# First loads of a fused attention and feed-forward kernel dealt out anew over two DMA queues

## The chip, the cores and the metric

The kernel runs on one core of a Trainium2 chip. The metric is the device time of one execution in microseconds; lower is better. Three runs of the kernel before the change gave 213.14, 213.52 and 213.74 us, so the median is 213.52 us.

## What is computed

A sequence of 2048 rows with 512 columns in bf16 is normalized row by row. The normalized rows go two ways. One is a sliding attention with 32 heads of 16 columns, where each row looks at itself and at 7 earlier rows at steps of 2. The other is a gated feed-forward layer with 1792 inner columns. The result is the input plus the attention's output times the silu of the feed-forward's output.

```python
xn = _layernorm(x, axis=-1)                      # x: 1 x 2048 x 512
s = _A_ref(xn, A_wqkv, A_wo)                     # q, k, v = xn @ wqkv; 8 keys per row; ... @ wo
g = _silu(_B_ref(xn, B_w_gate, B_w_up, B_w_down))  # (gelu(xn @ w_gate) * (xn @ w_up)) @ w_down
return x + s * g
```

## The kernel before

The 2048 rows are worked on in four blocks (j = 0 to 3) of 512 rows; a block has four tiles of 128 rows. For each block the kernel normalizes and transposes the rows (xnT), makes q, k and v, multiplies q with the shifted keys on VectorE (logits), takes the softmax, multiplies with the shifted values on VectorE, passes the result o through DRAM to turn it around (line 989 on), and multiplies it with wo (s_ps, line 1021). Beside that TensorE makes g and u (line 900) and y (line 960) of the feed-forward part. All matmuls of blocks 1 to 3 have 512 columns; those of q, k and v of block 0 are made tile by tile with 128 columns (`qkv_tiles`, line 584), so that they can begin when the first 128 rows are there.

**How the order of the work comes about.** Nothing is put in order by the hardware. Each step is an `Op` with an engine, an estimated duration, the names of the steps that it needs (a "~" in front means: needs only the start of that one) and a priority. `schedule` (line 126) plays the program through with fixed estimates of durations and of DMA times, always takes the step that can begin first, and among those within 0.05 us the one with the lowest priority. The order found this way is the order of the instructions on each engine. The numbers in `PARAMS` (base priorities N, S, V, Q, F, Y, O for the blocks and one `nudge` for each step) move the priorities, so other numbers give another order of the same steps.

**The first loads.** `loads` (line 1106) makes a list of DMAs, each of which may only be issued after the one before it in the list. SyncE (SP) issues all of them but three, which ScalarE's (ACT's) sequencer issues. In order: tile 0's rows in two column halves (ld_x0_0a on SP, ld_x0_0b on ACT), tile 1's rows in two column halves (both on SP), wq in two halves of 256 KB (ld_wqa and ld_wq, both on ACT), wk in two halves (ld_wka and ld_wk, both on SP), tiles 2 and 3 in one DMA of 256 KB (ld_x2_0, SP), wv in two halves (SP), and then, all on SP, the rows of block 1, the gate and up weights, and the rest. Below, "wka" and "wkb" are the first and the second half of wk, and the same for wq.

**The start of block 0.** Tiles 0 and 1 are normalized in column halves by `early_tile`: statistics (line 429), their sum (432), the root on ScalarE (435), reciprocal (440), the two normalized halves (444), two transposes each on TensorE (452), and copies out of PSUM (459 and 461). Then TensorE multiplies tile 0 with the first half of wq ("q0a", 8 matmuls), with the second ("q0b"), with wka ("k0a") and with wkb ("k0b"); tile 1's q ("q1a", "q1b") is cut in the same way, and all other tiles take 16 matmuls in one step. `preset` (line 264) is a square root of one column that ScalarE runs early, so that the table of that function is loaded before the first root needs it; it may not come ahead of the start of ld_wqa. `warm` (line 254) runs matmuls on zeros until the first rows are there.

**The end of blocks 0 to 2.** For a whole block at once, VectorE multiplies s16 (the evacuated s_ps) with the silu (line 1046), a DMA issued by GpSimd adds x (line 1049), and two DMAs of 256 KB, issued by SP, write the result to DRAM (line 1055). There is one buffer s16; block 1 can write into it (line 1036) when block 0's stores have read it.

Of the kernel before, what the change touches and what calls it, by code (L numbers as in the profile page):

```python
# [16 lines left out]
P = 128  # L17
# [4 lines left out]
TQ = 512  # L22
# [7 lines left out]
B, S, D, DF = 1, 2048, 512, 1792  # L30
NC = D // P
NF = DF // P
NJ = S // TQ
TPB = TQ // P
# [26 lines left out]
    sums=(3,), psum=(0,), warm=4, slack=3.5, N=[267.5, 33.2, 480.8, 875.4], S=[194.3, -690.4, 43.8, -317.7],  # L61
    V=[-45.5, -104.1, 270.7, -195.0], Q=[-3.6, -356.0, 73.8, 32.5], F=[86.8, 80.1, 275.5, 543.3],
    Y=[-111.3, 10.6, -115.3, -110.9], O=[33.1, -472.0, -324.1, 458.9], vnorm=(), vcopy=(2,), vsum=(0,),
    crowd=1.35,
    nudge=[
# [162 lines left out]
class Kernel:  # L228
# [33 lines left out]
    def preset(self):  # L262

        self.op("preset", "ACT", 0.2, ["warm0", "~ld_wqa"], lambda: self.nc.scalar.activation(
            out=self.spare[:], in_=self.eps[:], func=AF.Sqrt), prio=-1e6, table="sqrt")
# [16 lines left out]
    def layernorm(self, j):  # L282
        base = self.when("N", j)
        for tt in range(TPB):
            t = j * TPB + tt
# [89 lines left out]
            else:  # L375
                self.op(f"stats{t}", "DVE", 0.61,
                        [f"ld_x{j if j else 2}_{j}"] + {2: ["copy1"], 3: ["~aggr2"]}.get(t, ["~rstd3"]), stats, prio=prio,
# [631 lines left out]
    def out(self, j):  # L1009
# [32 lines left out]
        if j < NJ - 1:  # L1042
# [9 lines left out]

            def store(i, j=j):
                a = j * TQ + i * 2 * P
                self.nc.sync.dma_start(
                    out=self.out2d[a : a + 2 * P, :].rearrange("(t p) d -> p t d", p=P),
                    in_=self.t[f"s16{j}"][:, 2 * i : 2 * i + 2, :],
                )
# [5 lines left out]
            for i in range(2):  # L1064
                self.op(f"store{j}_{i}", "SP", 0.35, [f"add{j}"], lambda i=i, f=store: f(i), use=[f"s16{j}"],
                        nbytes=P * TPB * D, kind="out")
# [39 lines left out]
    def loads(self, src):  # L1106
        A_x, A_wqkv, A_wo, w_gate, w_up, w_down = src

        def x_tile(t, a=0, b=D, eng="sync"):
            getattr(self.nc, eng).dma_start(  # L1110
                out=self.x_sb[:, t, a:b], in_=A_x[0][t * P : (t + 1) * P, a:b]
            )
# [6 lines left out]
        def w_qkv(i, a=0, b=NC, eng="sync"):  # L1119
            getattr(self.nc, eng).dma_start(  # L1120
                out=self.w_sb[i][:, a:b, :],
                in_=A_wqkv.rearrange("(k p) n -> p k n", p=P)[:, a:b, i * D : (i + 1) * D],
            )
# [11 lines left out]
        def w_o():  # L1135
# [3 lines left out]
        kb = 1024  # L1139
        early = [(f"ld_x{t}_0{'ab'[i]}",  # L1140
                  lambda t=t, i=i: x_tile(t, i * D // 2, (i + 1) * D // 2, "sync" if t or not i else "scalar"),
                  64 * kb if t else kb) for t in range(2) for i in range(2)]
        h = NC // 2
        wq = [("ld_wqa", lambda: w_qkv(0, 0, h, "scalar"), 256 * kb), ("ld_wq", lambda: w_qkv(0, h, NC, "scalar"), 256 * kb)]
        wk = [("ld_wka", lambda: w_qkv(1, 0, h), 256 * kb), ("ld_wk", lambda: w_qkv(1, h, NC), 256 * kb)]
        wv = [("ld_wva", lambda: w_qkv(2, 0, h), 256 * kb), ("ld_wv", lambda: w_qkv(2, h, NC), 256 * kb)]
        x23 = [("ld_x2_0", lambda: x_block(2, 4), 256 * kb)]
        xb = [(f"ld_x{j}_{j}", lambda j=j: x_block(j * TPB, (j + 1) * TPB), 512 * kb) for j in range(NJ)]
        seq = early + wq + wk + x23 + wv + [xb[1]]
# [124 lines left out]
```

## Time and profile before

| What | Value |
|---|---|
| Median of three runs | 213.52 us (213.14 to 213.74) |
| The profiled execution's own time | 213.6 us |
| Its span, first to last instruction | 211.8 us |
| TensorE (PE) busy | 206.1 us |
| VectorE (DVE) busy | 187.6 us |
| ScalarE (ACT) busy | 150.3 us |
| GpSimd (POOL) busy | 65.5 us |
| Granted TensorE clock, mean | 0.999 |

The span is the time between the first and the last instruction of the profiled execution; 1.8 us of its time lie around it. PE's weight loads (PEld) run beside the matmuls. A row of the timeline gives start, duration, engine, line of the kernel, operation, what is written and read, and how many instructions are merged in it; a "q" behind the engine's name marks a DMA that the engine's sequencer issues, and such a row's duration is that of issuing, not of the transfer. A row of the DMA view gives the size of one transfer and the time from issue to landing.

### The profile page before, as it was taken

The page shows a single profiled execution, that of the slowest core. Times are in us where ns is not written, and L with a number is a line of the kernel's source. Part 1 is how long each engine was busy: PE and PEld are TensorE (multiplying, and loading weights), DVE is VectorE, ACT ScalarE, POOL GpSimd, SP SyncE. Part 2 cuts the span into 40 slices and gives each one's busy share as a digit, 9 for nine tenths or more (in the row PEclk, how much of TensorE's full clock was granted, in tenths as well). Part 3 has the DMA queues.
Part 4 walks back from the last instruction along what each step waited for, and adds up shares of the span by engine and source line. Part 5 has one row for each costly group of instructions (what it writes and reads, how often), then busy time and mean ns, then how long its engine had stood idle before and what let it go on. Part 6 is the DMA issues. An engine that isn't in the chain of part 4 may idle for free.

```text
span 211.8 us, 3074 instructions
## 1 busy us (share of the span) xinstructions
PE 206.1 (97%) x1105; PEld 102.0 (48%) x1123; DVE 187.6 (89%) x218; ACT 150.3 (71%) x257; POOL 65.5 (31%) x107
## 2 busy tenths in 40 slices
PE   7999999999999999999999999999999999999994
PEld 2896443445444444444444444444444444444442
DVE  4788998869999998999999999999999999997024
ACT  3587957999999899766905489966614489859051
POOL 5034200002115787440459520479730011001000
PEclk9999999999999999999999999999999999999999
DMA  5999999203802888962898865358797069708903
GB/s 182 348 382 373 298 280 240 50 3 74 173 25 73 186 135 144 178 192 38 144 114 135 166 173 115 99 99 162 143 192 163 0 104 231 163 0 149 249 4 99
DMA packets 33119, 32.17 MB, mean 152 GB/s; under 512 B 17088, under 2 KB 29648, under 8 KB 33104
## 3 DMA queue, kind: packets, MB, share of 16 engines
q0 software_dynamic: 5136, 14.41, 35.8%
q1 hardware_dynamic: 27136, 16.95, 31.0%
q10 hardware_dynamic: 832, 0.62, 1.0%
q8 instruction: 9, 0.15, 0.3%
q14 instruction: 6, 0.05, 0.1%
HBM read 14.12 MB, written 6.31 MB: 96 GB/s over the span
## 4 chain that ended last, share of the span: by engine, by line
PE 94%; DMA 2%; SPq 1%; issue 1%; DVE 0%; ACT 0%
PE g_ps L900 23%; PE y_ps L960 23%; PE u_ps L900 23%; PE qkv_ps L500 15%; PE s_ps L1021 6%; PE qkv_ps L584 5%; DMA wk_sb<-in_A_wqkv_dram 2%; SPq L1110 1%; PE L_ps L716 0%; PE tr_ps L345 0%; SPq L1120 0%; DVE s L1076 0%; ACT sil L976 0%; DVE s L1082 0%
## 5 line engine op out<-in xcount | busy, mean ns | idle before, releaser
L900 PE MATMUL g_ps<-xnT,wg_sb 128*128 128x512 bf16 x221 | 54.2, 379 | 0.2
L900 PE MATMUL u_ps<-xnT,wu_sb 128*128 128x512 bf16 x217 | 52.7, 379 | 0.3
L960 PE MATMUL y_ps<-wd_sb,hT 128*128 128x512 bf16 (+2 forms) x233 | 51.4, 366 | 0.2
L916 ACT ACTIVATE gl<-g_ps 128x512 bf16<-128x512 f32 x56 | 32.6, 598 | 18.6 <-PE g_ps L900 10.8
L772 POOL DMA_DIRECT2D Ls<-prod x48 | 36.3, 844 | 29.0 <-DMA Ls<-prod 9.8
L677 DVE TENSOR_TENSOR prod<-q_sb,k_sb 128x2048 bf16<-128x2048 bf16 x32 | 38.0, 1216 | 0.7 <-ACT q_sb L515 0.7
L924 ACT ACTIVATE hT<-u_ps 128x512 bf16<-128x512 f32 x56 | 32.4, 601 | 7.2 <-PE u_ps L900 6.6
L843 DVE TENSOR_TENSOR pv<-attn,v_arr 128x4096 bf16<-128x4096 bf16 x16 | 36.1, 2283 | 0.0
L960 PEld LDWEIGHTS <-hT 128*128 128x128 bf16 x238 | 22.8, 98 | 25.9
L900 PEld LDWEIGHTS <-wu_sb 128*128 128x128 bf16 x224 | 21.8, 98 | 26.6 <-issue 0.4
L900 PEld LDWEIGHTS <-wg_sb 128*128 128x128 bf16 x224 | 21.9, 98 | 26.2
L938 DVE TENSOR_TENSOR hT<-hT,gl 128x1024 bf16<-128x1024 bf16 x28 | 18.8, 683 | 1.3 <-ACT gl L916 1.1
L691 DVE TENSOR_TENSOR prod<-prod 128x2048 bf16<-128x2048 bf16 x16 | 19.2, 1214 | 0.0
L1021 PE MATMUL s_ps<-wo_sb,oT_sb 128*128 128x512 bf16 (+2 forms) x68 | 15.1, 366 | 0.1
L976 ACT ACTIVATE sil<-y_ps 128x512 bf16<-128x512 f32 (+2 forms) x17 | 9.1, 576 | 8.6 <-PE y_ps L960 8.5
L850 DVE TENSOR_TENSOR pv<-pv 128x2048 bf16<-128x2048 bf16 x12 | 14.3, 1215 | 0.0
L649 POOL DMA_DIRECT2D v_arr<-vT_dram x16 | 10.9, 700 | 10.4 <-DMA vT_dram<-vst 10.0
L866 POOL DMA_DIRECT2D pv<-pv x4 | 3.6, 894 | 30.6 <-DVE pv L843 30.1
L515 ACT ACTIVATE q_sb<-qkv_ps 128x512 bf16<-128x512 f32 x12 | 7.1, 624 | 8.2 <-PE qkv_ps L500 8.2
L1036 ACT ACTIVATE s<-s_ps 128x512 bf16<-128x512 f32 x15 | 8.9, 602 | 5.4 <-PE s_ps L1021 5.4
L500 PE MATMUL qkv_ps<-xnT,wv_sb 128*128 128x512 bf16 x48 | 12.3, 379 | 0.0
L542 POOL DMA_DIRECT2D vT_dram<-vst x12 | 7.2, 605 | 15.7 <-ACT vst L522 15.7
(91 smaller groups left out, 231.9 us busy)
## 6 DMA issues: line engine op xcount, KB each, us to landing
Ls<-prod POOLq DMA_DIRECT2D x48, 128.0 KB, 3.7
v_arr<-vT_dram POOLq DMA_DIRECT2D x16, 142.0 KB, 4.2
vT_dram<-vst POOLq DMA_DIRECT2D x16, 128.0 KB, 3.6
pv<-pv POOLq DMA_DIRECT2D x4, 512.0 KB, 5.4
oT_dram<-o_sb SPq DMA_DIRECT2D x16, 128.0 KB, 3.4
oT_sb<-oT_dram SPq DMA_DIRECT2D x4, 512.0 KB, 4.8
wg_sb<-in_B_w_gate_dram SPq DMA_DIRECT2D x2, 896.0 KB, 10.6
wu_sb<-in_B_w_up_dram SPq DMA_DIRECT2D x2, 896.0 KB, 12.5
```

The lines of the kernel that those rows point to most:

```text
L500: self.nc.tensor.matmul(ps[:], lhsT=self.w_qkv(which, dk, c), rhs=self.t[f"xT{j}"][:, dk, :], start=(dk == 0), stop=(dk == NC - 1),)
L677: self.nc.vector.tensor_tensor(out=self.t[pair][:, c % 2].rearrange("p n w t -> p w n t"), in0=q.unsqueeze(1).to_broadcast([P, W, 2, P]), ...
L691: self.nc.vector.tensor_tensor(out=pr[:, 0], in0=pr[:, 0], in1=pr[:, 1], op=ALU.add)
L772: self.nc.gpsimd.dma_start(out=self.t[f"Ls{j}"][H * tq : H * (tq + 1)], in_=self.t[f"pr{j}_{tq // 2}_0"][s::NC, 0, tq % 2], **(dict(accum_ ...
L843: self.nc.vector.tensor_tensor(out=pv[:], in0=self.t[f"at{j}"][:, 2 * i : 2 * i + 2, :].unsqueeze(2).to_broadcast([P, 2, DH, P]), in1=win, ...
L850: self.nc.vector.tensor_tensor(out=pv[:, 0], in0=pv[:, 0], in1=pv[:, 1], op=ALU.add)
L900: nc.tensor.matmul(ps[:], lhsT=w[:, dk, fc * P : (fc + 1) * P], rhs=self.t[f"xT{j}"][:, dk, :], start=(dk == 0), stop=(dk == NC - 1),)
L916: self.nc.scalar.activation(out=self.t[f"gl{j}_{pair}"][:, fc % 2, :], in_=self.t[f"ps_g{j}_{fc}"][:], func=AF.Gelu_apprx_tanh,)
L924: self.nc.scalar.activation(out=self.t[f"h{j}"][:, fc, :], in_=self.t[f"ps_u{j}_{fc}"][:], func=AF.Copy)
L938: self.nc.vector.tensor_tensor(out=h, in0=h, in1=self.t[f"gl{j}_{pair}"][:], op=ALU.mult)
L960: nc.tensor.matmul(self.t["ps_" + key][:, 0 : n1 - n0], lhsT=self.t[f"h{j}"][:, fc, tt * P : (tt + 1) * P], rhs=self.wd_sb[:, fc, n0:n1], ...
L1021: self.nc.tensor.matmul(ps[:, 0 : n1 - n0], lhsT=self.t[f"oT{j}"][:, c, tt * P : (tt + 1) * P], rhs=self.wo_sb[:, c, n0:n1], start=(c == 0 ...
```

## The change

Four things are changed.

1. The list of first loads: tile 1's halves go one to each queue, and so do the two halves of wq and of wk. The second half of wq moves from ACT to SP, and the first half of wk from SP to ACT. Tiles 2 and 3 are loaded by two DMAs of 128 KB in place of one of 256 KB, and tile 2's and tile 3's statistics each wait for their own.
2. `preset` may not come ahead of the start of ld_x1_0b (tile 1's second half, now on ACT) in place of ld_wqa.
3. Block 0's result is stored by one DMA of 512 KB in place of two of 256 KB; blocks 1 and 2 keep two.
4. All the numbers in `PARAMS` that set priorities are new: the base priorities, `slack` (3.42 for 3.5) and the whole list of nudges, so that the order of the steps can differ anywhere.

The estimates in `schedule` and the steps themselves are otherwise the same.

```diff
-    sums=(3,), psum=(0,), warm=4, slack=3.5, N=[267.5, 33.2, 480.8, 875.4], S=[194.3, -690.4, 43.8, -317.7],
-    V=[-45.5, -104.1, 270.7, -195.0], Q=[-3.6, -356.0, 73.8, 32.5], F=[86.8, 80.1, 275.5, 543.3],
-    Y=[-111.3, 10.6, -115.3, -110.9], O=[33.1, -472.0, -324.1, 458.9], vnorm=(), vcopy=(2,), vsum=(0,),
+    sums=(3,), psum=(0,), warm=4, slack=3.42, N=[236.5, 17.4, 498.7, 880.9], S=[216.5, -699.2, 31.7, -311.4],
+    V=[-49.3, -109.4, 272.5, -204.7], Q=[2.1, -363.3, 74.7, 33.2], F=[84.5, 80.7, 277.2, 546.4],
+    Y=[-118.9, 11.7, -116.0, -110.2], O=[36.5, -485.8, -342.3, 458.0], vnorm=(), vcopy=(2,), vsum=(0,),
...
-        self.op("preset", "ACT", 0.2, ["warm0", "~ld_wqa"], lambda: self.nc.scalar.activation(
+        self.op("preset", "ACT", 0.2, ["warm0", "~ld_x1_0b"], lambda: self.nc.scalar.activation(
...
-                        [f"ld_x{j if j else 2}_{j}"] + {2: ["copy1"], 3: ["~aggr2"]}.get(t, ["~rstd3"]), stats, prio=prio,
+                        [f"ld_x{j if j else t}_{j}"] + {2: ["copy1"], 3: ["~aggr2"]}.get(t, ["~rstd3"]), stats, prio=prio,
...
+            parts = 2 if j else 1
+            n = TPB // parts
+
             def store(i, j=j):
-                a = j * TQ + i * 2 * P
+                a = j * TQ + i * n * P
                 self.nc.sync.dma_start(
-                    out=self.out2d[a : a + 2 * P, :].rearrange("(t p) d -> p t d", p=P),
-                    in_=self.t[f"s16{j}"][:, 2 * i : 2 * i + 2, :],
+                    out=self.out2d[a : a + n * P, :].rearrange("(t p) d -> p t d", p=P),
+                    in_=self.t[f"s16{j}"][:, n * i : n * (i + 1), :],
                 )
...
+        def half_x(t, i, eng, size=64):
+            return (f"ld_x{t}_0{'ab'[i]}", lambda: x_tile(t, i * D // 2, (i + 1) * D // 2, eng), size * kb)
+
+        def half_w(w, i, eng):
+            return (f"ld_w{'qkv'[w]}" + "a" * (1 - i), lambda: w_qkv(w, i * h, (i + 1) * h, eng), 256 * kb)
+
+        early = [half_x(0, 0, "sync", 1), half_x(0, 1, "scalar", 1), half_x(1, 0, "sync"), half_w(0, 0, "scalar"),
+                 half_x(1, 1, "scalar"), half_w(0, 1, "sync"), half_w(1, 0, "scalar"), half_w(1, 1, "sync")]
+        early += [(f"ld_x{t}_0", lambda t=t: x_tile(t), 128 * kb) for t in (2, 3)]
+        early += [half_w(2, 0, "sync"), half_w(2, 1, "sync")]
```

More of the change, by code (lines that the diff above doesn't have):

```diff
@@ L1063, in out @@
                     nbytes=P * TPB * D * 2, kind="acc")
-            for i in range(2):
+            for i in range(parts):
                 self.op(f"store{j}_{i}", "SP", 0.35, [f"add{j}"], lambda i=i, f=store: f(i), use=[f"s16{j}"],
-                        nbytes=P * TPB * D, kind="out")
+                        nbytes=P * n * D * 2, kind="out")
             return
@@ L1139, in loads @@
         kb = 1024
-        early = [(f"ld_x{t}_0{'ab'[i]}",
-                  lambda t=t, i=i: x_tile(t, i * D // 2, (i + 1) * D // 2, "sync" if t or not i else "scalar"),
-                  64 * kb if t else kb) for t in range(2) for i in range(2)]
         h = NC // 2
[L1144 to L1147, printed above, removed]
+        def half_x(t, i, eng, size=64):
[6 more added lines that the diff above has]
+        early += [half_w(2, 0, "sync"), half_w(2, 1, "sync")]
         xb = [(f"ld_x{j}_{j}", lambda j=j: x_block(j * TPB, (j + 1) * TPB), 512 * kb) for j in range(NJ)]
-        seq = early + wq + wk + x23 + wv + [xb[1]]
+        seq = early + [xb[1]]
         seq += [("ld_wga", lambda: w_ff(w_gate, lambda: self.wg_sb, 0, half), 896 * kb)]
```

88 rows, old and new, of the table nudge are left out of this document.

## The prediction, made before the changed kernel ran

> **What bounds the kernel now.** I read the head of the page first, then the busy time by stages, then the chain of waits in order of time, and last the timeline of the stages that the change touches.
>
> ```profile
> span 211.8 us, 3074 instructions
> ...
> PE 206.1 (97%) x1105; PEld 102.0 (48%) x1123; DVE 187.6 (89%) x218; ACT 150.3 (71%) x257; POOL 65.5 (31%) x107
> ...
> PE 94%; DMA 2%; SPq 1%; issue 1%; DVE 0%; ACT 0%
> ```
>
> PE is busy for 97% of the span and holds 94% of the chain that ended last. The stages say where the rest is; the columns are stretch, its length, busy time (and instructions) of PE, PEld, DVE, ACT and POOL, granted clock, busy share of the DMA engines, GB/s.
>
> ```profile
> 3.00:5.00 2.00, 2.00 (x8) 0.65 (x6) 1.91 (x7) 0.52 (x3) 1.00 (x10) 1.00 0.99 308
> 5.00:6.50 1.50, 1.28 (x13) 0.99 (x13) 1.27 (x6) 0.67 (x2) 0.00 (x0) 1.00 1.00 309
> 6.50:8.00 1.50, 1.40 (x24) 1.23 (x22) 0.53 (x3) 0.60 (x1) 0.00 (x0) 1.00 1.04 352
> ...
> 18.00:100.00 82.00, 81.58 (x379) 37.91 (x385) 77.59 (x87) 70.86 (x125) 25.88 (x38) 1.00 0.69 149
> 100.00:195.00 95.00, 94.53 (x434) 43.66 (x441) 94.00 (x86) 64.47 (x104) 34.44 (x46) 1.00 0.68 129
> 195.00:205.00 10.00, 9.95 (x49) 4.62 (x48) 0.05 (x1) 2.76 (x5) 0.00 (x0) 1.00 0.58 152
> ```
>
> From 18 to 205 us PE idles 0.42 + 0.47 + 0.05 = 0.94 us in all. No order of the steps can win more than that there, so a gain has to come from the start or the end. The chain shows both:
>
> ```profile
> 2.68 5.27 DMA wk_sb<-in_A_wqkv_dram
> ...
> 8.00 3.31 PE qkv_ps L584 x56
> ...
> 208.46 0.29 ACT sil L976
> ...
> 209.09 0.23 DVE s L1082
> ```
>
> The last thing that PE waits for is wkb: issued at 2.68, landed at 2.68 + 5.27 = 7.95 us; from 8.00 us on it is PE's own work to the end. The end (silu, gate, add, store from 208.46 us) isn't touched by the change.
>
> ```profile
> 5.78 1.45 PE L584 MATMUL qkv_ps<-xnT,wq_sb 128*128 128x128 bf16 x16 [0.22 <-ACT xnT L459]
> 7.07 0.61 PE L584 MATMUL qkv_ps<-xnT,wk_sb 128*128 128x128 bf16 x8
> 7.51 0.39 PE L452 MATMUL tr_ps<-ident,xn 128*128 128x128 bf16 x4
> ...
> 8.47 0.61 PE L584 MATMUL qkv_ps<-xnT,wq_sb 128*128 128x128 bf16 x8
> ...
> 10.26 1.06 PE L584 MATMUL qkv_ps<-xnT,wv_sb 128*128 128x128 bf16 x16
> ```
>
> Starts tell the pace better than the modelled ends. Eight matmuls of 128 columns take 7.51 - 7.07 = 0.44 us and four transposes half of that, 0.22; so the transposes are through at 7.73, and PE stands still until 8.00: **0.27 us**. That is all that an earlier wk can win, against 213.6 us of this execution. The 16 matmuls of q0 take 7.07 - 5.78 = 1.29 us where 16 at the later pace take 0.89, so 0.4 us go there to a slower PE, though the granted clock reads 1.00. The Trainium skill ("TensorE: Matmul & The Clock Gate", Part 1) has matmuls at half pace until a free-running activity window of about 3.4 us has passed; by that rule these 0.4 us could shrink or grow by a few tenths with the window's phase, without any cause in the change.
>
> **The change part by part: the loads.** Here are issues and landings of before; a DMA row's last number is the time to landing.
>
> ```profile
> 0.82 1.34 SPq L1110 DMA_DIRECT2D x_sb<-in_A_x_dram  x3
> 1.81 0.43 ACTq L1120 DMA_DIRECT2D wq_sb<-in_A_wqkv_dram  x1
> 2.20 0.94 SPq L1120 DMA_DIRECT2D wk_sb<-in_A_wqkv_dram  x2
> 3.19 0.47 SPq L1115 DMA_DIRECT2D x_sb<-in_A_x_dram  x1
> ```
>
> ```profile
> x_sb<-in_A_x_dram SPq DMA_DIRECT2D x1, 64.0 KB, 3.2
> wq_sb<-in_A_wqkv_dram ACTq DMA_DIRECT2D x1, 256.0 KB, 3.8
> wk_sb<-in_A_wqkv_dram SPq DMA_DIRECT2D x1, 256.0 KB, 4.1
> x_sb<-in_A_x_dram SPq DMA_DIRECT2D x1, 256.0 KB, 5.3
> ```
>
> The three SP issues of x take 1.34 us, so x1's second half goes out at about 1.73 and lands 3.2 later, near 4.9. wqb lands at 1.81 + 3.8 = 5.6, wka at 2.20 + 4.1 = 6.3, tiles 2 and 3 at 3.19 + 5.3 = 8.5 us. These landings follow the order of issue across both queues, not two streams side by side. From 3 to 8 us the 16 DMA engines are busy all the time (shares 0.99, 1.00, 1.04). So bytes ahead of a load decide: x0, x1, wq and wk are 128 + 128 + 512 + 512 = 1280 KB, and all of these lie ahead of the end of wk before and after. **wkb gains nothing: 7.95 us as before.** The Trainium skill ("DMA: Bandwidth & Descriptors", section "Issuing engines are not separate DMA queues") says the same: DMAs issued from several engines run on the same 16 engines, and only issue time is saved; by that the change's dealing out wins 0 us, and if it were wrong the sum would be rival 1 below. The busy shares agree.
>
> **wka loses.** Before, its 256 KB went ahead of wkb's. Now wka is ACT's fourth DMA, one issue behind its third (1.81 + 0.43, so about 2.25), and wkb is SP's fourth (2.20, the place that wka had): both go out together, share the engines, and land at nearly one time. Bounds for wka: 6.3, as before, and 7.95, as wkb. Both compete over the whole stretch, so I take a value near the later end, **7.6**. PE then idles from 7.07 until 7.6. If it stays with the order k0a, transposes of tile 1, k0b, q1a: k0a 7.65 to 8.10, transposes to 8.32, k0b to 8.77, and q1a begins at 8.77 in place of 8.47: +0.30. If the new priorities put the transposes first, they lie in the gap, and 16 matmuls from 7.65 end at 8.54: +0.07. Bounds: with wka at 7.95 and the old order 8.00 + 0.44 + 0.22 + 0.44 = 9.10, so +0.63; with wka at 6.3 and wkb early enough, -0.27. I take **+0.2**, between the two orders.
>
> **x1's second half** moves behind wqa and beside wqb: 768 KB lie ahead of its end, where wqb was before (5.6). So it lands between 4.9 and 5.6 us.
>
> ```profile
> 5.02 0.42 DVE L429 BATCH_NORM_STATS2 stats<-x_sb 128x6 f32<-128x256 bf16 x1
> ...
> 6.25 0.60 DVE L444 TENSOR_SCALAR xn<-x_sb,mv,rstd 128x256 bf16<-128x256 bf16 x2
> ...
> 7.83 0.49 DVE L461 COPY xnT<-tr_ps 128x256 bf16<-128x256 bf16 x2 [0.97 <-PE tr_ps L452]
> 8.48 0.69 DVE L291 BATCH_NORM_STATS2 stats<-x_sb 128x6 f32<-128x512 bf16 x1 [0.16 <-DMA x_sb<-in_A_x_dram]
> ```
>
> At worst tile 1's statistics begin at 5.6 in place of 5.02, the normalized halves end at 6.85 + 0.6 = 7.45 in place of 6.85. Before, the transposes began at 7.51 only because PE was at k0a, so 7.45 is still early enough: **0**. Behind the waiting statistics on DVE stands tile 0's second copy, for q0b, which PE reaches in the second half of its 1.29 us; should it come up to 0.3 us late there, PE's wait for wka behind it takes that up. **Tiles 2 and 3 apart**: one SP issue more (0.47 us), but SP has six issues ahead of wv before and after, so wv isn't later. Tile 2's 128 KB land some 0.35 us earlier (half of 256 KB at 352 GB/s), so DVE's 0.16 us of waiting at 8.48 goes; PE takes tile 2 only behind the row of 10.26, with work that is there: **0**.
>
> **preset** and ACT's fourth issue:
>
> ```profile
> 1.74 1.28 ACT L264 ACT_TABLE_LOAD   x1 [1.74 <-PEq L1258]
> ...
> 3.04 0.20 ACT L264 ACTIVATE spare<-eps 128x1 f32<-128x1 f32 x1
> 3.98 0.29 ACT L435 ACTIVATE rstd<-mv,eps 128x1 f32<-128x1 f32 x1 [0.74 <-DVE mv L432]
> ```
>
> The table load moves behind one more issue of 0.43 us: 2.2 to 3.5, the root of one column to 3.7. The first root waits for DVE until 3.98, so 0.74 us of cover shrink to 0.3: **0**. If preset slipped by a further issue, 0.15 us of it would delay all that follows.
>
> **Block 0's store in one.**
>
> ```profile
> 124.34 0.90 SPq L1055 DMA_DIRECT2D out_dram<-s  x2
> 150.71 4.35 SPq L993 DMA_DIRECT2D oT_dram<-o_sb  x4
> ```
>
> ```profile
> L1036 ACT ACTIVATE s<-s_ps x4: 597/597/597, 168.1 to 171.1; 128x512 bf16<-128x512 f32 x4
> ```
>
> One issue of 0.45 us goes. SP has nothing to do until 150.71, and s16 is written again only at 168.1: **0**, with tens of us of cover.
>
> **The new priorities** change the order everywhere; no row of before shows the new one. Above: at most the 0.94 us of idle time can go. Below: what a badly timed step costs is rival 2. I take 0, nearest to the rows, since the same estimates of durations that made the order of before left 0.94 us idle in 187.
>
> **Sum**: 213.6 + 0.2 = 213.8 us for an execution like the profiled one, which lies 0.08 above the median of 213.52; so **213.7 us**. A difference under 0.3%, 0.64 us, is about what a measurement here can't tell from none.
>
> **The rivals.** *1. Two queues do bring wk earlier.* Should both halves be there at 7.07 to 7.7 us, the 0.27 us go: 213.3. For it: DMA moves 308 GB/s from 3 to 5 us and 352 later, so the early stretch has some slack. Against it: the full shares, and landings in order of issue.
>
> *2. The new order makes VectorE late (slower).* DVE is 99% busy from 100 to 195 us, so a delay before that isn't made up.
>
> ```profile
> 189.15 1.22 DVE L855 TENSOR_TENSOR o_sb<-pv 128x2048 bf16<-128x2048 bf16 x1
> ...
> 195.69 0.37 SPq L1002 DMA_DIRECT2D oT_sb<-oT_dram  x1
> ...
> 203.26 2.75 PE L1021 MATMUL s_ps<-wo_sb,oT_sb 128*128 128x512 bf16 x12
> ```
>
> ```profile
> DMA to landing us min/median/max: 4.7/4.7/4.7
> ```
>
> The last attention block is done on DVE at 190.4; it is turned through DRAM and back at 195.69 + 4.7 = 200.4, and PE takes it at 203.26. So DVE may be 2.9 us late; from there on each us is a us of the total, since PE has no other work left. In the stretch from 18 to 100 us DVE idles 4.4 us; an order that doubles this makes the end 4.4 - 2.9 = 1.5 us later: 215.2. For it: every priority is new. Against it: the margin.
>
> *3. wka's issue stands behind preset on ACT's stream.* Then it goes out at about 3.7 and lands, like the x of tiles 2 and 3, 5.3 us later, at 9.0. With all of tile 1's q drawn ahead, k0 ends at 9.0 + 0.9 = 9.9, where the same set of steps took until 8.47 + 0.44 + 0.45 = 9.36: +0.5. In the old order q1a begins at 9.0 + 1.1 = 10.1 in place of 8.47: +1.6. In the middle about 1 us: 214.7. Against it: wqb was issued at 1.81, while preset's own root ran only at 3.04.
>
> **How the numbers follow.** Chances: forecast 0.47, rival 1 0.18, rival 2 0.27, rival 3 0.08. Faster by over 0.3% (below 212.9) needs more than the idle time of the start: 0.05, mostly from rival 1. Slower (above 214.2): 0.25 from rival 2, 0.07 from rival 3, 0.03 from the forecast's upper end, 0.35 in all. Within: 0.60. The range runs from 212.9 (rival 1 with a lucky start) to 215.2 (rival 2's price). The forecast's own range is 213.3 to 214.2.
>
> **What would show it.** Right: wka and wkb land within 0.5 us of each other between 7.3 and 8.1, PE idles before its first wk matmul, and the later stages have PE busy as now. Wrong: wkb lands before 7.5 (rival 1); a stretch after 18 us in which PE idles over 0.5 us, or s_ps of the last block waiting for oT (rival 2); the wka issue after 3.5 us (rival 3).

## The result and the profile after

The changed kernel takes **214.83 us** (median of 10 runs, 214.53 to 216.21), the kernel before beside it 213.50 (10 runs, 213.14 to 214.18). The ratio is 1.0064, 95% interval 1.0047 to 1.0081: slower, by more than the 0.3% that a measurement tells from none. The forecast was 213.7, with a change of less than 0.3% as the likeliest case. That case does not hold. The time lies inside the range given (212.9 to 215.2), but above the forecast's own range (213.3 to 214.2).

The profiled execution took 214.61 us with a span of 212.6, against 213.6 and 211.8 before. The head of the page of the changed kernel:

```profile
span 212.6 us, 3071 instructions
...
PE 205.8 (97%) x1105; PEld 101.9 (48%) x1123; DVE 187.9 (88%) x218; ACT 150.7 (71%) x257; POOL 65.4 (31%) x107
...
PE 94%; DMA 2%; ACTq 1%; issue 1%; ACT 0%; DVE 0%
```

PE still holds 94% of the chain. What is new is that the chain's start runs over ACT's queue (ACTq) in place of SP's. The busy time by stages of the changed kernel (columns as before: stretch, length, PE, PEld, DVE, ACT, POOL, granted clock, DMA share, GB/s) says where PE idles:

```profile
6.50:8.00 1.50, 0.61 (x8) 0.45 (x7) 0.77 (x3) 0.75 (x2) 0.00 (x0) 1.00 1.09 372
...
18.00:100.00 82.00, 81.58 (x389) 38.36 (x396) 76.80 (x86) 71.05 (x127) 25.96 (x38) 1.00 0.69 149
100.00:195.00 95.00, 94.53 (x433) 43.64 (x441) 94.33 (x86) 64.28 (x104) 34.29 (x46) 1.00 0.70 128
195.00:205.00 10.00, 9.95 (x49) 4.66 (x49) 0.74 (x2) 2.89 (x4) 0.00 (x0) 1.00 0.66 164
```

From 18 to 205 us PE is busy 81.58, 94.53 and 9.95 us, to the hundredth what it was before. From 6.5 to 8.0 us it is busy 0.61 us where it was 1.40. The chain of waits of the changed kernel, in order of time, names the cause of that gap:

```profile
2.25 0.61 ACT L266
2.86 5.24 DMA wk_sb<-in_A_wqkv_dram
8.10 0.05 issue
8.15 0.64 PE qkv_ps L586 x8
...
209.28 0.29 ACT sil L978
```

The last load that PE waits for is now **wka**, issued at 2.86 and landed at 8.10 us. The end begins at 209.28 in place of 208.46: +0.82 us. PE's timeline at the start shows the same amount:

```profile
5.76 1.38 PE L586 MATMUL qkv_ps<-xnT,wq_sb 128*128 128x128 bf16 x16 [0.26 <-ACT xnT L461]
8.15 0.64 PE L586 MATMUL qkv_ps<-xnT,wk_sb 128*128 128x128 bf16 x8 [1.01 <-DMA wk_sb<-in_A_wqkv_dram]
8.62 0.39 PE L454 MATMUL tr_ps<-ident,xn 128*128 128x128 bf16 x4
8.85 0.61 PE L586 MATMUL qkv_ps<-xnT,wk_sb 128*128 128x128 bf16 x8
9.29 0.61 PE L586 MATMUL qkv_ps<-xnT,wq_sb 128*128 128x128 bf16 x8
```

The steps have the same order as before (q0, k0a, transposes, k0b, q1a). k0a begins 8.15 - 7.07 = 1.08 us later, the wait of 0.27 us for wkb is gone, and q1a begins at 9.29 in place of 8.47: +0.82. So the whole difference of the two spans arises before 9.3 us, in one wait of 1.01 us. Why wka is late stands in the timeline of all engines:

```profile
2.19 0.47 SPq L1125 DMA_DIRECT2D wk_sb<-in_A_wqkv_dram  x1
2.25 1.28 ACT L266 ACT_TABLE_LOAD   x1 [2.25 <-issue]
...
2.70 0.47 SPq L1115 DMA_DIRECT2D x_sb<-in_A_x_dram  x1
2.86 0.39 ACTq L1125 DMA_DIRECT2D wk_sb<-in_A_wqkv_dram  x1
2.86 0.43 DVE L431 BATCH_NORM_STATS2 stats<-x_sb 128x6 f32<-128x256 bf16 x1 [1.65 <-DMA x_sb<-in_A_x_dram]
```

ACT's queue is free at 1.73 + 0.49 = 2.22 us, but wka goes out only at 2.86. That is the very moment at which DVE gets tile 0's first half. In the compiled program the issue carries a wait for that load. A semaphore is a counter that a DMA raises when its data have landed; the DMAs that SP and ACT issue report to eight of them, dealt out in turn. By the program's order the eight loads from x0 to wkb and tile 2 take the first round; tile 3's issue and wka's are the ninth and the tenth, and must wait until the loads that used their semaphores have landed. So wka comes out behind tile 2's load (2.70) and its 128 KB. The DMA view of the changed kernel (size, time to landing):

```profile
wk_sb<-in_A_wqkv_dram SPq DMA_DIRECT2D x1, 256.0 KB, 4.2
x_sb<-in_A_x_dram SPq DMA_DIRECT2D x2, 128.0 KB, 4.7
wk_sb<-in_A_wqkv_dram ACTq DMA_DIRECT2D x1, 256.0 KB, 5.2
```

wkb, issued in wka's old place, lands at 2.19 + 4.2 = 6.4 us, far earlier than before, and is of no use there: PE takes k0a first, and wka comes at 8.1.

### The profile page after: what moved, and what is told of

It reads as the page before. It is cut to its first block, busy times and chain, and to the rows that moved or that the text cites. A ratio compares the mean times of both kernels' runs of the same rounds, so it can differ in the third digit from the quotient of the medians.

```text
span 212.6 us, 3071 instructions
## 1 busy us (share of the span) xinstructions
PE 205.8 (97%) x1105; PEld 101.9 (48%) x1123; DVE 187.9 (88%) x218; ACT 150.7 (71%) x257; POOL 65.4 (31%) x107
## 4 chain that ended last, share of the span: by engine, by line
PE 94%; DMA 2%; ACTq 1%; issue 1%; ACT 0%; DVE 0%
PE g_ps L902 23%; PE y_ps L962 23%; PE u_ps L902 23%; PE qkv_ps L502 15%; PE s_ps L1023 6%; PE qkv_ps L586 5%; DMA wk_sb<-in_A_wqkv_dram 2%; ACTq L1115 0%; ACT L266 0%; PE L_ps L718 0%; ACTq L1125 0%; PE tr_ps L347 0%; DVE s L1081 0%; ACT sil L978 0%; DVE s L1087 0%
## 5 line engine op out<-in xcount | busy, mean ns | idle before, releaser
L902 PE MATMUL g_ps<-xnT,wg_sb 128*128 128x512 bf16 x220 | 53.0, 379 | 0.3
L978 ACT ACTIVATE sil<-y_ps 128x512 bf16<-128x512 f32 (+2 forms) x17 | 9.7, 586 | 9.3 <-PE y_ps L962 9.2
L502 PE MATMUL qkv_ps<-xnT,wk_sb 128*128 128x512 bf16 x47 | 12.1, 379 | 0.1
L502 PE MATMUL qkv_ps<-xnT,wq_sb 128*128 128x512 bf16 x46 | 11.7, 379 | 0.1
```

Of the source, the lines that this page charges most:

```text
L502: self.nc.tensor.matmul(ps[:], lhsT=self.w_qkv(which, dk, c), rhs=self.t[f"xT{j}"][:, dk, :], start=(dk == 0), stop=(dk == NC - 1),)
L902: nc.tensor.matmul(ps[:], lhsT=w[:, dk, fc * P : (fc + 1) * P], rhs=self.t[f"xT{j}"][:, dk, :], start=(dk == 0), stop=(dk == NC - 1),)
```

## The experiments

My theory behind the result: **wka's place alone** (on ACT, behind x2 and the semaphore) makes the kernel slower. The rivals: the new priorities or another part cost something too; the table load of preset holds the issue; the first trace of before was no typical one. Unless another kernel is named, the diffs are against the changed kernel.

### Old queues, everything else new

```diff
-                 half_x(1, 1, "scalar"), half_w(0, 1, "sync"), half_w(1, 0, "scalar"), half_w(1, 1, "sync")]
+                 half_x(1, 1, "sync"), half_w(0, 1, "scalar"), half_w(1, 0, "sync"), half_w(1, 1, "sync")]
```

> The changed kernel with its new priorities, x2 and x3 apart and the single store, but x1's second half, wq and wk on the queues of before (x1b and both halves of wk on SP, both halves of wq on ACT). Theory (the place of wk's first half in the order of issue makes the whole loss, the new priorities cost nothing): wka lands near 6.3 us, wkb near 8.0, tile 1's q begins near 8.5 us in place of 9.29, the span is 211.8 us and the time that of the kernel before within 0.3 us (213.3 to 213.8). Rival (part of the loss comes from the new priorities or the single store): the start is as before, but the time stays over 214.1.

Measured: 213.29 us (11 runs), ratio to before 0.9999 (0.9984 to 1.0013). The new priorities, the single store of block 0 and the parted loads of tiles 2 and 3 together cost nothing and win nothing. The chain and a stage of this kernel:

```profile
2.67 4.90 DMA wk_sb<-in_A_wqkv_dram
```

```profile
18.00:100.00 82.00, 82.00 (x387) 37.95 (x385) 76.83 (x87) 71.05 (x125) 25.20 (x37) 1.00 0.67 149
```

Two things can be seen here beside the verdict. wkb, issued as before at 2.67, lands at 2.67 + 4.90 = 7.57, not at 7.95. And PE is busy 82.00 of 82 us: this trace has all 1123 matmuls, while the first ones of before and after have 1105 records. The idle time of 0.94 us that I read there was missing records.

### Only wka back on SP

```diff
-                 half_x(1, 1, "scalar"), half_w(0, 1, "sync"), half_w(1, 0, "scalar"), half_w(1, 1, "sync")]
+                 half_x(1, 1, "scalar"), half_w(0, 1, "sync"), half_w(1, 0, "sync"), half_w(1, 1, "sync")]
```

> The changed kernel with one thing undone: both halves of wk on SP. x1's second half stays on ACT and wq's second half on SP. Theory (only wk's first half is misplaced; x1 and wq moved cost nothing): wka is issued near 2.2 and lands near 6.5, wkb near 7.7, PE goes from q0 at 7.0 into k0a without a wait and waits only for wkb; tile 1's q begins near 8.2, and the time is that of before within 0.3 us (213.1 to 213.7). Rival (x1's second half, 0.6 us later, delays tile 1 and the second half of q0 enough to be seen): 0.3 to 0.6 us above before.

Measured: 213.34 us (11 runs), ratio 0.9997 (0.9987 to 1.0006). The cost is gone with this one word. In PE's timeline no wait for wk is left:

```profile
6.86 0.61 PE L586 MATMUL qkv_ps<-xnT,wk_sb 128*128 128x128 bf16 x8
...
7.55 0.61 PE L586 MATMUL qkv_ps<-xnT,wk_sb 128*128 128x128 bf16 x8
8.00 0.61 PE L586 MATMUL qkv_ps<-xnT,wq_sb 128*128 128x128 bf16 x8
```

So x1's second half and wq's second half may change queues at no cost in sum, and the best dealing-out ties with the kernel before. It is not free of waits: q0 takes 6.86 - 5.76 = 1.10 us, against 6.54 - 5.61 = 0.93 in the first experiment, because its second half waits for DVE's copy (done at 6.13 + 0.24 = 6.37), which stands behind x1's second half (5.5 us). In return wkb lands at about 2.7 + 4.5 = 7.2 us, before PE reaches it; with the old queues it landed at 7.46 to 7.95. This is one trace, so whether the dealing-out or the scatter of landings does that is open. No version that I ran beats the kernel before.

### The two halves of wk exchanged

```diff
-                 half_x(1, 1, "scalar"), half_w(0, 1, "sync"), half_w(1, 0, "scalar"), half_w(1, 1, "sync")]
+                 half_x(1, 1, "scalar"), half_w(0, 1, "sync"), half_w(1, 0, "sync"), half_w(1, 1, "scalar")]
```

> The changed kernel with the two halves of wk exchanged between the queues: the first, which PE takes first, on SP, the second on ACT. Theory: the half on SP lands near 6.4 and the one on ACT near 8.1, whichever half it is; PE goes through q0 to 7.0, takes k0a without a wait, then waits for wkb until 8.15, and tile 1's q begins near 8.6: 0.1 to 0.2 us slower than before, 213.6 to 213.8. Rival (both halves share the engines and land together): wka lands after 7.5, tile 1's q begins after 8.9, time over 214. Rival of the priorities: over 214.1 in spite of the earlier start.

Measured: 214.10 us (5 runs), ratio 1.0037 (1.0025 to 1.0049), slower than expected. The mechanism is the one expected: the half on ACT's queue is the late one, whichever half it is. ACT issues wkb at 2.83 and it lands at 8.26, while k0a runs at 6.82 without a wait.

```profile
6.82 0.61 PE L586 MATMUL qkv_ps<-xnT,wk_sb 128*128 128x128 bf16 x8
...
8.30 0.64 PE L586 MATMUL qkv_ps<-xnT,wk_sb 128*128 128x128 bf16 x8 [0.63 <-DMA wk_sb<-in_A_wqkv_dram]
```

The expectation was too low for two reasons: q1a begins at 8.78 and not near 8.6, and the expectation reckoned from the first trace of before (q1a at 8.47), where wkb landed late; in the second (below) q1a begins at 8.16.

### The wait taken away: preset behind wka

The order is changed so that ACT issues wka ahead of preset; the semaphores are then dealt out anew.

```diff
+    names = [o.name for o in order]
+    o = order.pop(names.index("preset"))
+    order.insert([o.name for o in order].index("ld_wka") + 1, o)
```

> The changed kernel with preset's square root moved behind the issue of wk's first half on ACT. In the program this issue then waits for no earlier DMA's semaphore, and x2's waits in its place. Theory (the wait for x0's landing, until 2.84 us, holds the issue at 2.86 and lets x2 go ahead): wka is issued near 2.25, ahead of x2, and lands between 7.2 and 7.7 in place of 8.10, so PE's wait shrinks by 0.4 to 0.9 us; the table load now ends near 4.0, so tile 0's root may come up to 0.3 us late. Time 0.3 to 0.7 us below the changed kernel's: 214.1 to 214.5. Rival (the table load itself holds the issue, or the two queues simply share the engines): wka lands at 7.9 or later again and the time stays within 0.2 us of the changed kernel's.

Measured: 214.30 us (median of 8 runs, 213.51 to 216.91); the ratio, 1.0039 (1.0024 to 1.0054), is without the longest run, whose mean granted clock is 0.990. The timeline of its first profile:

```profile
2.25 0.46 ACTq L1125 DMA_DIRECT2D wk_sb<-in_A_wqkv_dram  x1
...
2.74 1.28 ACT L266 ACT_TABLE_LOAD   x1 [2.74 <-issue]
...
3.12 0.34 SPq L1115 DMA_DIRECT2D x_sb<-in_A_x_dram  x1
```

wka is issued at 2.25; now tile 2's load on SP waits until 3.12, when tile 0's other half has landed. For wka this is the arrangement that my prediction had assumed, and still the kernel costs 0.4%. It is not a clean test of wka alone: preset runs one issue later, so tile 0's root starts at 4.14 in place of 3.89 us and q0 at 5.92 in place of 5.76, about the 0.15 us that the prediction names for this. In the executions timed, 213.5 to 213.9 and 214.3 to 214.5 both occur, so I profiled it once more.

> The kernel of e3 again, for a second trace, since its runs lie at 213.5 and at 214.3 to 214.5 us and its one trace belongs to the lower group. Theory (wka's landing decides): in a run of the upper group wka lands 0.5 us or more later than the 6.92 of the first trace. Rival (the table load): wka lands near 6.9 again, and what is late in the upper group is tile 0's root or PE's clock.

Measured: 214.33 us. The chain of this second profile:

```profile
2.26 5.56 DMA wk_sb<-in_A_wqkv_dram
...
7.86 0.64 PE qkv_ps L586 x8
```

wka lands at 7.82 (6.92 in the first profile, issued at the same time), and q1a begins at 9.00 rather than 8.11. wkb lands at 2.20 + 4.3 = 6.5 us in the first profile and at 2.20 + 5.4 = 7.6 in the second. So two halves issued together land within 0.5 us of each other, and when they do varies by about 1 us between these two executions. In the second, preset's later root is hidden behind the wait for wka.

### Only the queues new, in the kernel before

The old priorities with the new queues (against the kernel before); tiles 2 and 3 stay one load, so that 256 KB stand ahead of wka.

```diff
-                  lambda t=t, i=i: x_tile(t, i * D // 2, (i + 1) * D // 2, "sync" if t or not i else "scalar"),
+                  lambda t=t, i=i: x_tile(t, i * D // 2, (i + 1) * D // 2, "scalar" if i else "sync"),
...
-        wq = [("ld_wqa", lambda: w_qkv(0, 0, h, "scalar"), 256 * kb), ("ld_wq", lambda: w_qkv(0, h, NC, "scalar"), 256 * kb)]
-        wk = [("ld_wka", lambda: w_qkv(1, 0, h), 256 * kb), ("ld_wk", lambda: w_qkv(1, h, NC), 256 * kb)]
+        wq = [("ld_wqa", lambda: w_qkv(0, 0, h, "scalar"), 256 * kb), ("ld_wq", lambda: w_qkv(0, h, NC), 256 * kb)]
+        wk = [("ld_wka", lambda: w_qkv(1, 0, h, "scalar"), 256 * kb), ("ld_wk", lambda: w_qkv(1, h, NC), 256 * kb)]
...
+    o = order.pop([o.name for o in order].index("ld_x1_0b"))
+    order.insert([o.name for o in order].index("ld_wqa") + 1, o)
```

> The kernel before with its own priorities, tiles 2 and 3 in one DMA and two stores of block 0, but with the queues of the changed kernel: x1b and wka on ACT, wqb on SP, preset behind x1b. wka's issue now waits for x0's landing and goes out near 3.0, behind tiles 2 and 3. Theory: wka lands at 8.1 or a little later, tile 1's q begins 0.8 to 1.1 us later than before, and the time is 0.7 to 1.2 us above before, as much as the changed kernel. Rival of the priorities: under 0.5 us above before.

Measured: 216.68 us (6 runs, 214.63 to 217.01), ratio 1.0128 (1.0089 to 1.0167): the sign holds, the size is missed. wka, issued at 2.97 behind 256 KB, lands at 9.03. Four of the six executions have a mean granted clock of 0.990 to 0.992 and spans of 214.9 to 215.3, two have 0.999 and 212.9 to 213.0. PE's timeline and the stages of a profile of the first kind (the column behind POOL is the granted clock):

```profile
9.07 1.04 PE L584 MATMUL qkv_ps<-xnT,wk_sb 128*128 128x128 bf16 x8 [1.89 <-DMA wk_sb<-in_A_wqkv_dram]
...
11.19 0.99 PE L584 MATMUL qkv_ps<-xnT,wq_sb 128*128 128x128 bf16 x8
```

```profile
7.00:9.00 2.00, 0.19 (x4) 0.03 (x1) 0.54 (x2) 0.60 (x1) 0.00 (x0) 0.89 1.06 348
9.00:10.00 1.00, 0.93 (x9) 0.93 (x10) 0.00 (x0) 0.00 (x0) 0.00 (x0) 0.50 1.08 378
10.00:11.00 1.00, 1.00 (x13) 1.00 (x11) 0.64 (x3) 0.00 (x0) 0.00 (x0) 0.50 1.08 388
11.00:12.00 1.00, 1.00 (x12) 1.00 (x11) 0.96 (x3) 0.57 (x2) 0.00 (x0) 0.51 1.06 382
12.00:13.00 1.00, 1.00 (x21) 1.00 (x19) 0.86 (x4) 0.21 (x2) 0.00 (x0) 1.00 1.06 382
```

After 1.89 us without a matmul PE runs at half the clock from 9 to 12 us: 13 and 12 matmuls in each of the last two of these microseconds, then 21. That is a second price, on top of the wait.

### The wait filled with matmuls

Against the kernel of the last experiment; the added matmuls on zeros are work that the kernel does not need.

```diff
+                    if key == "k0_t0" and a == 0:
+                        for _ in range(8):
+                            self.nc.tensor.matmul(
+                                ps[:].rearrange("p c t -> p (c t)"), lhsT=self.blank[:, 0:P], rhs=self.blank[:],
+                                start=True, stop=True,
+                            )
```

> The kernel of e4 (queues of the changed kernel alone) with eight matmuls of 512 columns on zeros put in front of k0a, into the bank that k0a then overwrites: extra work of 1.7 us that lies in PE's wait for wka. Theory (in e4 the wait of 2 us let the granted clock fall to one half for 3 us, and that is most of its loss over the changed kernel): PE is busy through the wait, the clock stays at 1.00, k0a begins near 9.1, and the time is 214.5 to 214.9, 1.7 to 2.2 us below e4 although more is computed. Rival (the wait itself makes e4's loss): the time stays at 216 or more.

Measured: 215.61 us (6 runs, 215.22 to 216.44), ratio 1.0106 (1.0088 to 1.0125), clock 0.998 to 1.0 in every one. PE's timeline:

```profile
6.92 1.89 PE L584 MATMUL qkv_ps<-blank 128*128 128x512 bf16 x8
9.04 0.64 PE L590 MATMUL qkv_ps<-xnT,wk_sb 128*128 128x128 bf16 x8 [0.23 <-DMA wk_sb<-in_A_wqkv_dram]
...
10.18 0.61 PE L590 MATMUL qkv_ps<-xnT,wq_sb 128*128 128x128 bf16 x8
```

wka lands as late as before (8.99) and q1a begins at 10.18, where it began at 11.19 with the empty wait. More work, and 1.07 us faster by the medians: the half clock was caused by the empty wait. The two executions of the empty wait that kept the clock (214.63 and 214.76 us) are faster than all with the wait filled; they have no trace, so whether wka came earlier in them is open. The expected time was too low, though k0a began at 9.04 as expected (near 9.1): q1a comes 10.18 - 8.16 = 2.02 us later than in the second trace of before, and about that much is lost (215.61 against 213.47, the median of before beside it).

### GpSimd's zeros out of the way

Does the early store of zeros on GpSimd's queue make one of wk's packets late? Against the first experiment, it goes out behind the store of the first v.

```diff
-    nc.gpsimd.dma_start(
-        out=k.vT.rearrange("(c p) s -> p c s", p=P)[:, :, 0:PAD], in_=vzero[:]
-    )
...
+        if o.name == "st_v0_0":
+            nc.gpsimd.dma_start(
+                out=k.vT.rearrange("(c p) s -> p c s", p=P)[:, :, 0:PAD], in_=vzero[:]
+            )
```

> The kernel of e1 (new priorities, queues of before) with GpSimd's small DMA of zeros into the front of v's DRAM buffer issued behind tile 0's v near 13 us, in place of 2.4 us. Theory of the straggler (some of the 16 DMA engines fall behind because of these small packets, and wkb waits for the slowest): wkb lands before 7.3 in place of 7.56, PE's only wait at the start shrinks to under 0.1 us, and the time is 0.2 to 0.4 us below before: 212.9 to 213.1. Rival (the bytes ahead of wk decide): wkb lands at 7.5 or later, the time stays within 0.15 us of before.

Measured: 213.66 us (12 runs), ratio 1.0009 (0.9989 to 1.0029), wkb landed at 7.46. No gain is seen, and wkb lands hardly earlier than the 7.57 of the first experiment; that theory falls. Why the landing varies by some tenths between executions stays open.

### Both kernels profiled once more

> The kernel before, unchanged, for a second trace. In e1, which has its queues, the second half of wk landed at 7.56 us, 0.4 us earlier than in the one trace of before (7.95). Theory (that trace was a late one, and counting the change's loss from it made the loss look smaller): wkb lands between 7.2 and 7.7 and tile 1's q begins between 7.9 and 8.3 us, with a span of 211.2 to 211.6. Rival (new priorities or x2 and x3 apart make e1's wk earlier): wkb lands near 7.95 again.

> The changed kernel, unchanged, for a second trace. Theory (x0's landing holds wka's issue, x2 goes ahead): wka is issued between 2.8 and 2.95, behind x2 at 2.70, lands between 8.0 and 8.4, and tile 1's q begins between 9.2 and 9.6 us. Rival (the first trace was an unusual one): wka is issued near 2.25 or lands before 7.8.

Measured: before 213.38 us, span 211.4; after 214.86, span 212.7. The chain of before:

```profile
2.20 4.53 DMA wk_sb<-in_A_wqkv_dram
...
7.64 0.05 issue
7.69 1.36 PE qkv_ps L584 x21
```

PE's timeline of before:

```profile
7.25 0.39 PE L452 MATMUL tr_ps<-ident,xn 128*128 128x128 bf16 x4
...
8.16 0.61 PE L584 MATMUL qkv_ps<-xnT,wq_sb 128*128 128x128 bf16 x8
```

PE's timeline of after:

```profile
8.30 0.64 PE L586 MATMUL qkv_ps<-xnT,wk_sb 128*128 128x128 bf16 x8 [0.64 <-DMA wk_sb<-in_A_wqkv_dram]
...
9.45 0.61 PE L586 MATMUL qkv_ps<-xnT,wq_sb 128*128 128x128 bf16 x8
```

Before, the transposes are through at 7.25 + 0.22 = 7.47, PE waits some 0.2 us for wkb, which lands at 7.64, and q1a begins at 8.16; after, wka lands at 8.26 and q1a begins at 9.45. That is 1.29 us, and the spans differ by 1.3, as the medians do (214.83 - 213.50 = 1.33). So this pair, and not the first (0.82 us), is the typical one: 19 executions of before timed with the first four experiments have a median span of 211.4 us, 23 timed with later ones 211.6, and the ten of the changed kernel 212.8.

All traces together show where the difference lies. In eleven of the twelve the span less the start of q1a is 203.2 to 203.3 us (before 211.8 - 8.47, after 212.6 - 9.29), with old and new priorities, one store and two. Only the trace with the half clock has more, 214.9 - 11.19 = 203.7. So the start of q1a is the whole difference, and what the change does behind it costs and wins nothing.

## Why the prediction was right and where it was wrong

The time lies inside the range by luck: its upper end, 215.2, was the price of rival 2, which did not happen. The parts that I put at 0 are 0 in sum; one term, wka's, was too small.

- **"A gain has to come from the start or the end": right.** It holds even more strictly than I wrote: the 0.94 us between 18 and 205 us were missing records. The second traces of both kernels, with all 1123 matmuls, have PE busy for all of these 187 us. With the best queues (only wka back on SP) the time is that of before.
- **"wkb gains nothing, 7.95 us as before": right in the sum, wrong in the landing.** wkb lands at 6.4 us, because it now has the place in the order of issue that wka had, and wka lands last. The end of wk as a whole does not come earlier: 8.10 and 8.26 us, against 7.95 and 7.64. With 372 GB/s between 6.5 and 8 us and a full share of the DMA engines, dealing the bytes over two queues moved none of them faster in these traces. The Trainium skill ("DMA: Bandwidth & Descriptors", section "Issuing engines are not separate DMA queues") says that only time of issue is saved; these landings agree with it.
- **"wka loses, +0.2": the step that failed, in size.** It measured +0.82 in the first pair of traces and +1.29 in the second. First, I had it issued at 2.25; it went out at 2.86 (2.94 in the second trace), because its issue waits for tile 0's load, and behind tile 2's 128 KB. Those take 128 KB / 372 GB/s = 0.35 us, so that the end of wk comes at 7.64 + 0.35 = 8.0 us or later, above my upper bound of 7.95. Second, I took a landing between "alone" and "shared" (7.6) and averaged over two orders on PE; the order stayed the old one. Third, the trace that I started from had a late wkb (7.95 against 7.64 us): q1a began at 8.47, against 8.16 in the second one, so a loss reckoned from it comes out 0.3 us smaller. Without the late issue the loss is still 0.39% (preset behind wka), part of it from preset's later root.
- **The 0.4 us of a slower PE in q0: they did shrink, and did not count.** The row of q0 reads 1.45 us in the first trace of before and 1.05 in the second; k0a begins at 7.07 and 6.78, but q1a follows wkb's landing in both.
- **x1's second half, 0: right.** It landed at 5.6 us and DVE waited 0.63 us for it; in the second trace it landed at 6.0, later than the 5.6 that I gave as the latest, and DVE waited 0.92 us. The second half of q0 then starts late (DVE's copy for it ends at 6.24 + 0.24 = 6.48, q0's first half at about 5.76 + 0.44 = 6.20), and the wait for wka behind it takes that up, as predicted.

```profile
5.65 0.43 DVE L431 BATCH_NORM_STATS2 stats<-x_sb 128x6 f32<-128x256 bf16 x1 [0.63 <-DMA x_sb<-in_A_x_dram]
```

  With only wka back on SP there is such a wait too (0.48 us); PE loses some 0.2 us to it there and gets them back from wkb's earlier landing, and the time is that of before.
- **Tiles 2 and 3 apart, the new priorities, preset's smaller cover, block 0's store: 0, right.** The first, second and fourth stand in the first experiment, preset's place in the second (its rule is new there, and the time is 213.34). The store's issue of 0.38 us in place of 0.90 stands where SP has nothing else for 26 us (changed kernel):

```profile
125.45 0.38 SPq L1060 DMA_DIRECT2D out_dram<-s  x1
151.51 0.58 SPq L995 DMA_DIRECT2D oT_dram<-o_sb  x1
```

- **Rival 1, two queues bring wk earlier: false**, as said. **Rival 2, the new order makes VectorE late: false.** In the changed kernel oT of the last block is fetched at 195.87 us and PE takes it at 204.08; these lie 8.21 us apart, against 7.57 before, so the margin has grown:

```profile
195.87 0.37 SPq L1004 DMA_DIRECT2D oT_sb<-oT_dram  x1
```

```profile
204.08 2.75 PE L1023 MATMUL s_ps<-wo_sb,oT_sb 128*128 128x512 bf16 x12
```

- **Rival 3, wka's issue held on ACT: nearest to the truth**, and with 214.7 us near the time, but with another holder. The table load does not hold the queue: in the changed kernel wka goes out at 2.86 while the load runs from 2.25 to 3.53. What preset's place decides is which semaphore wka gets. The release is seen in five traces. Where the semaphore is that of tile 0's first half, the issue starts with DVE's first statistics (2.86, 2.83, 2.94). In the two kernels with the old priorities it is the second half's, which lands at 2.95 and 3.07, and wka goes out at 2.97 and 3.09.
- **"wka and wkb land within 0.5 us of each other": false** in both traces of after (6.4 and 8.1; 6.6 and 8.3), true in both profiles with preset behind wka (6.5 and 6.92; 7.60 and 7.82), where both go out together as I had assumed.

## What to carry to other kernels

When the DMA engines are full, as here from 3 to 8 us, look at the order of issue over both queues: it decided who waited, and the half that is used first should be issued first. The second queue won no time here. Ask of every moved DMA not only when its queue is free but what else its issue waits for: in this program a DMA beyond the first round of eight completion semaphores waits for an older load to land, and a neighbour on the other queue slipped ahead of it. And before a wait of some tenths of a microsecond is counted as a possible gain, profile the kernel before twice: here the landing of one load varied by 0.3 to 0.4 us, and a loss has to be reckoned from the typical trace.

## What the runs showed of the hardware that was not expected

A wait of 1.89 us was enough for the granted clock to fall to 0.50 for about 3 us (seen in one trace of the kernel with only the queues new; four of its six executions have the low mean clock and spans 2 us longer). Eight matmuls on zeros in the wait kept it at 1.00. The Trainium skill ("TensorE: Matmul & The Clock Gate", Part 1) gives the fall only after an idle window of about 3.4 us; these rows differ, and the measurement decides. One of the ten runs of the changed kernel, with its wait of about 1 us, took 216.21 us at a mean clock of 0.992; that this was the same fall is only argued, since that run has no trace. The same holds for the run of 216.91 us with preset behind wka (0.990).

The time from issue to landing of the same 256 KB, issued at the same moment, scattered by 0.9 us (wka, 6.92 and 7.82) and 1.1 us (wkb, 6.5 and 7.6) where two loads were issued together, and by 0.3 us where they followed one another (wkb 7.64 and 7.95 in the two traces of before). Why is open.
